# Sliding-window attention with a feed-forward block: batch 3's k moved from TensorE transposes to a transposing DMA

## The chip, the core and the metric

One core of a Trainium2 chip runs the whole kernel. Its engines each execute their own instructions in order: TensorE (PE in the profile; PEld is its weight load), VectorE (DVE), ScalarE (ACT), GpSimd (POOL) and SyncE (SP), which here only issues DMAs. The metric is the device time of one execution in microseconds (us); less is better. A measurement of this kernel can tell about 0.2% from no change.

## The reference

```python
# q, k, v: (8 batches, 8 heads, 576 tokens, 64)
scores = scale * np.matmul(q, k.transpose(0, 1, 3, 2))
mask = (rel >= 0) & (rel < 128)              # rel = query position - key position
scores = np.where(mask, scores - slopes * np.abs(rel), -1e9)
attn = softmax(scores); attn_out = np.matmul(attn, v)
x = attn_out.transpose(0, 2, 1, 3).reshape(4608, 512)
h = x @ w_in                                 # 512 -> 2048
g = h * np.clip(h + 3.0, 0.0, 6.0) / 6.0
return g @ w_out                             # 2048 -> 512
```

## The kernel before

**Units of work.** Attention is done for g = 0 to 31, a pair of heads each: g = 4 * batch + pair. The feed-forward block goes by tiles of 512 tokens (nt = 0 to 8): for each tile 16 "up" units (L532, four matmuls into hps, then ACT and DVE make gbuf) and 16 "down" units (L587, four matmuls into ops; every fourth ends a block of 128 rows, which DVE copies to osb and SyncE writes out, L597). Tile 3 covers tokens 1536 to 2047, that is the end of batch 2 and the most of batch 3. Four consecutive matmuls of an up unit read xT for head pairs 0, 1, 2, 3.

**Order.** The order on every engine is the order of the program, written by hand. `segment` runs iterations g = 8 to 32: scores(g) on TensorE, exp_diag and exp_off (ACT makes pd, po and p4buf, GpSimd masks them, L427, L436, L442), values(g - 1) (TensorE, then DVE divides into avs, L474), back(g - 1), stage_next(g), and between these `fill(n)`, which hands out n units of the feed-forward block. An up unit is only handed out once all pairs of its batches have been written to xT in the program's order.

**q and k.** Scores need q and k with the 64 channels of two heads on the partitions (qTb, kTb, two of each, by turns of the batch). There are two ways. By *doubles*: load_double (L105) brings runs of 9 tokens, GpSimd casts them (prepare_double, L246), TensorE transposes (double, L269, 5 and 4 transposes) and ACT or DVE copies the result (L271). By *token blocks and a transposing DMA*: load_block (L117) brings blocks of 128 tokens (five for a tensor, the last one half), GpSimd casts them into tbuf (cast_tokens, L213), and one transposing DMA, issued by SyncE (xbar, L218), writes qTb or kTb. Before the change batch 2 and batch 3's k go by doubles, batch 3's q and all of batches 4 to 7 by token blocks, with one tbuf for q and k.

**v and the values.** v is loaded by token blocks too and cast by GpSimd into vbuf (L206, L209). back(g) (L510) writes avs into xT by a transposing DMA on SyncE for g >= 8, other than g = 10 and 11, which go over TensorE and ACT (L517, L519).

**Queues.** All loads in the steady part, the transposing DMAs and the outputs leave through SyncE's one queue, in program order; a load whose room is not free, or a transposing DMA whose cast is not done, holds those behind it. Four ldbuf take turns: q3 is in ldbuf3, k3 in ldbuf1, v3 in ldbuf0. `LOADS` says in which iteration's stage_next a tensor is loaded ("q4" is batch 4's q).

Of the kernel before, what the change touches and what calls it, by code (L numbers as in the profile page):

```python
# [11 lines left out]
BF16 = mybir.dt.bfloat16  # L12
# [6 lines left out]
def kernel(  # L19
# [9 lines left out]
    nc = tc.nc  # L29
# [35 lines left out]
    held = ctx.enter_context(tc.tile_pool(name="held", bufs=1))  # L65
    prs = ctx.enter_context(tc.tile_pool(name="prs", bufs=2))
    ppool = ctx.enter_context(tc.tile_pool(name="ppool", bufs=2))
    small = ctx.enter_context(tc.tile_pool(name="small", bufs=2))
    rpool = ctx.enter_context(tc.tile_pool(name="rpool", bufs=2))
    opool = ctx.enter_context(tc.tile_pool(name="opool", bufs=4))  # L70
# [2 lines left out]
    ps_h = ctx.enter_context(tc.tile_pool(name="ps_h", bufs=2, space=bass.MemoryType.PSUM))  # L73
    ps_o = ctx.enter_context(tc.tile_pool(name="ps_o", bufs=1, space=bass.MemoryType.PSUM))

    tbuf = held.tile([128, NP, NQ, 128], BF16, name="tbuf")
    ldbuf = [held.tile([128, NQ * H * D], FP32, name=f"ldbuf{i}") for i in range(4)]
    gbuf = [held.tile([128, n_ms, NT], BF16, name=f"gbuf{i}") for i in range(2)]
    vbuf = [held.tile([128, NQ, H, W], BF16, name=f"vbuf{i}") for i in range(2)]
# [35 lines left out]
    def load_block(b, nm, j, eng):  # L115
        n = min(128, S - j * 128)
        eng.dma_start(out=tokens(b, nm)[:n, j, :, :],  # L117
                      in_=src_of[nm][b, :, ds(j * 128, n), :].rearrange("h p d -> p h d"))
# [32 lines left out]
    def memsets_later():  # L151
        for i in range(2):
            nc.gpsimd.memset(p4buf[i], 1.0)
        nc.gpsimd.memset(kTb[1][:, :, 4, LAST:128], 0.0)
        nc.gpsimd.memset(vbuf[1][:, :, :, D:W], 1.0)
        nc.gpsimd.memset(vbuf[1][64:128, 4, :, 0:D], 0.0)
        nc.gpsimd.memset(tbuf[64:128, :, 4, :], 0.0)

    def warm_up(n):
        w = ps_av.tile([128, 4, 128], FP32, tag="av", name="w")  # L160
# [41 lines left out]
    def cast_tokens(b, nm):  # L202
        s = ld[b, nm]
        if nm == "v":
            for lo in (0, 2):
                nc.gpsimd.tensor_copy(  # L206
                    out=vbuf[b % 2][:, lo:lo + 2, :, 0:D].rearrange("p j h d -> p (j h) d"),
                    in_=s[:, lo:lo + 2, :, :].rearrange("p j h d -> p (j h) d"))
            nc.gpsimd.tensor_copy(out=vbuf[b % 2][:LAST, 4, :, 0:D], in_=s[:LAST, 4, :, :])  # L209
            return  # L210
        for j in range(NQ):
            m = min(128, S - j * 128)
            nc.gpsimd.tensor_copy(out=tbuf[:m, :, j, :],  # L213
                                  in_=s[:m, j, :, :].rearrange("p (i e) d -> p i (e d)", e=2))

    def xbar(b, nm):
        dst = (qTb if nm == "q" else kTb)[b % 2]
        nc.sync.dma_start_transpose(out=dst.rearrange("p h j c -> p (h j) c"),  # L218
                                    in_=tbuf.rearrange("p h j c -> p (h j c)"))

    st = {}

# [243 lines left out]
    def values(g, qts):  # L466
        av = ps_av.tile([128, 3, 2, W], FP32, tag="av", name="av", padded_shape=[128, 3, 2, 85])
        nq = len(qts)
        av_matmuls(g, qts, lambda qt, e: av[:, qt - qts[0], e, :])
        if qts[0] == 0:  # L470
            st[g, "avs"] = small.tile([128, NQ, 2, D], BF16, tag="avs", name="avs")
        rc = small.tile([128, 3, 2, 1], FP32, tag="rc", name="rc")
        nc.vector.reciprocal(rc[:, 0:nq, :, :], av[:, 0:nq, :, D:W])
        nc.vector.tensor_tensor(  # L474
            out=st[g, "avs"][:, qts[0]:qts[0] + nq, :, :], in0=av[:, 0:nq, :, 0:D],
            in1=rc[:, 0:nq, :, :].to_broadcast([128, nq, 2, D]), op=ALU.mult)

    def attend(g):
        wide = score_banks()
        av = wide[:, :, 0:NQ * W].rearrange("p e (j c) -> p e j c", j=NQ)  # L480
        av_matmuls(g, range(NQ), lambda qt, e: av[:, e, qt, :])
        avs = st[g, "avs"] = small.tile([128, NQ, 2, D], BF16, tag="avs", name="avs")
        rc = small.tile([128, 2, NQ, 1], FP32, tag="rcw", name="rcw")
        nc.vector.reciprocal(rc, av[:, :, :, D:W])
        nc.vector.tensor_tensor(out=avs.rearrange("p j e d -> p e j d"), in0=av[:, :, :, 0:D],  # L485
                                in1=rc.to_broadcast([128, 2, NQ, D]), op=ALU.mult)

    def attend_split(g, tags):
        st[g, "avs"] = small.tile([128, NQ, 2, D], BF16, tag="avs", name="avs")
# [119 lines left out]
    def fill(n):  # L609
        for _ in range(n):  # L610
# [3 lines left out]
            if fn is moe_up and done[0] < NP * (min((nt * NT + NT - 1) // S, B - 1) + 1):  # L614
# [3 lines left out]

    V, P, A = nc.vector.tensor_copy, nc.gpsimd.tensor_copy, nc.scalar.copy

    LOADS = {9: "v3", 10: "q4", 12: "k4", 13: "v4", 14: "q5", 16: "k5", 17: "v5", 18: "q6",
             20: "k6", 21: "v6", 22: "q7", 24: "k7", 25: "v7"}

    VCAST = {15: 4, 19: 5, 23: 6, 27: 7}
# [1 line left out]
    def stage_next(g):  # L626
        b, hp = divmod(g, NP)
        nb = b + 1
        if g == 2 * NP:
            cast_tokens(2, "v")  # L630
        late = nb > 3 and hp == 1
        for n in LOADS.get(g, "").split():
            for j in range(3 if late else NQ):
                load_block(int(n[1]), n[0], j, nc.sync)
        if nb == 3 and hp < 2:
            prepare_double(3, hp, (P,), "k")
        if nb == 3 and hp == 1:
            cast_tokens(3, "q")
            xbar(3, "q")
        elif nb < B and nb > 3 and hp < 2:  # L640
            cast_tokens(nb, "qk"[hp])
            xbar(nb, "qk"[hp])
        for n in LOADS.get(g, "").split() if late else ():
            for j in range(3, NQ):
                load_block(int(n[1]), n[0], j, nc.sync)
        if VCAST.get(g):
            cast_tokens(VCAST[g], "v")

# [80 lines left out]
    def second_batch():  # L729
        scores_diag(NP + 0)  # L730
        exp_diag(NP + 0, 0)
        exp_diag(NP + 0, 1)
        up_begin(0, 2, n_ks, "av")
        scores_off(NP + 0)
        exp_off_full(NP + 0)
        wide_double(1, 1, "k", V)
        fill(2)
        scores_diag(NP + 1)
        exp_diag(NP + 1, 0)
        exp_diag(NP + 1, 1)  # L740
# [24 lines left out]
        load_w_out(2)  # L765
        load_w_out(3)
        prepare_double(2, 1, (P, P))
        nc.gpsimd.memset(ldbuf[2][:, 0:1], 0.0)
        load_tokens(2, "v")
        for dp in range(2):  # L770
            load_double(3, dp, "k", nc.sync)
        load_tokens(3, "q")
        up_begin(0, 13, n_ks)
        attend(NP + 1)
        back(NP, "o")
        attend(NP + 2)
# [17 lines left out]
    def segment(lo, hi, fills):  # L794
        for g in range(lo, hi + 1):
# [2 lines left out]
                done[0] = g - 1  # L798
            if lo < g < hi and g != 3 * NP + 1:
                scores(g)  # L800
            turn = {2 * NP: (2, 1, "k"), 2 * NP + 1: (2, 1, "q"),
                    2 * NP + 2: (3, 0, "k"), 2 * NP + 3: (3, 1, "k")}.get(g)
            if turn:
                double(*turn, 0, "av", A)
            fill(f[0])
            if turn:
                double(*turn, 1, *(("h", V) if turn[0] == 2 else ("av", A)))
            if g < hi:
                exp_diag(g, 0)
            fill(f[1])  # L810
# [76 lines left out]
```

## Time and profile before

| | |
|---|---|
| median of three runs | 319.51 us (319.5 to 320.04) |
| profiled execution | 319.64 us |
| its span in the profile | 317.9 us |
| TensorE busy | 307.0 us |
| SyncE transposing DMAs for q and k (L218) | 9, issue 3.7 to 4.8 us each |
| loads of 256 KB by token blocks | packets of 256 B |
| loads of 288 KB by doubles | packets of 2304 B |

All times below count from the start of the span; the execution's own time is 1.7 us longer. In a timeline, a row is: start, duration, engine, line and operation, what it writes and reads, how many were merged. The duration of a DMA row on SyncE is the time in which SyncE is occupied with issuing it, not the transfer; the trace also has a landing record for each DMA, the moment when its last part arrived. Iterations begin, by scores on TensorE, at 59.97 (g = 9), 67.98 (10), 75.90 (11), 84.11 (12), 88.03 (13), 96.04 (14), 103.21 (15), 111.24 (16) and 119.28 (17).

Landing records of the DMAs that the prediction speaks of (last part, us):

```
v2 blocks       58.02 58.97 60.05 61.23 62.06
k3, doubles     62.64 63.38 64.74 65.58
q3 blocks       66.79 68.05 70.39 71.93 72.79
v3 blocks       74.93 76.11 77.29 78.51 79.24
q3 transposed   82.77
back(9)         83.71
q4 blocks       85.72 86.82 88.02 89.42 89.76
k4 blocks       92.93 94.11 96.24 97.26 97.70
q4 transposed   99.98
k4 transposed   110.24
v4, last block  111.49
q5, last block  118.59
back(14)        120.47
back(15)        121.48
back(19)        153.26
```

### The profile page before, as it was taken

To read this page: it belongs to the slowest core of one execution; us is meant where nothing else is said; L and a number is where in the kernel's file an instruction comes from. 1 tells how busy PE (TensorE), PEld (TensorE's weight loads), DVE (VectorE), ACT (ScalarE), POOL (GpSimd) and SP (SyncE) were. 2 spreads that over 40 slices of the span, in tenths; PEclk is the share of its full clock that TensorE was granted. 3 is DMA by queue.
4 is the path that set the end of the run, shared out by engine and by line. 5 is a ranking of instruction groups with operands and counts; after the bars stand their busy time and mean duration, and the time that the engine had idled before them with its cause. 6 is when DMAs were issued, how large, how long until landed. Compare 5 with 4: busy or idle time off the path is not lost.

```text
span 317.9 us, 6980 instructions
## 1 busy us (share of the span) xinstructions
PE 307.0 (97%) x2671; PEld 163.4 (51%) x2710; DVE 176.1 (55%) x344; ACT 196.8 (62%) x338; POOL 138.9 (44%) x247
## 2 busy tenths in 40 slices
PE   8889999999999999999999999999999999999996
PEld 3565474455554445555676644454444444444443
DVE  6677676554456654566465546564656455455510
ACT  3869986877767666766667756675764244244401
POOL 7358192674594684548463854472231000000000
PEclk9999999999999999999999999999999999999999
DMA  7999999999999999999999999934112100000112
GB/s 271 264 373 215 255 236 200 236 235 198 216 265 180 222 215 212 213 196 253 186 178 219 190 206 198 228 95 57 49 29 75 66 34 33 35 33 33 66 57 77
DMA packets 131425, 52.43 MB, mean 165 GB/s; under 512 B 118976, under 2 KB 122816, under 8 KB 131392
## 3 DMA queue, kind: packets, MB, share of 16 engines
q1 hardware_dynamic: 125648, 46.15, 69.0%
q0 software_dynamic: 3696, 3.67, 7.1%
q10 hardware_dynamic: 2048, 2.16, 2.2%
q8 instruction: 21, 0.34, 0.5%
q14 instruction: 12, 0.10, 0.1%
HBM read 36.70 MB, written 9.44 MB: 145 GB/s over the span
## 4 chain that ended last, share of the span: by engine, by line
PE 90%; ACT 3%; DVE 3%; issue 2%; POOL 0%; DVEq 0%; POOLq 0%; ACTq 0%
PE hps L532 38%; PE ops L587 37%; PE score L399 3%; PE av L463 2%; PE av L455 2%; DVE avs L485 1%; PE ops L568 1%; PE w L163 1%; ACT w_out_sb L422 1%; PE score L346 1%; PE tp L269 1%; ACT r L556 1%; DVE gbuf L557 1%; PE score L301 1%; PE score L357 1%
## 5 line engine op out<-in xcount | busy, mean ns | idle before, releaser
L556 ACT ACTIVATE r<-hps,bias 128x512 f32<-128x512 f32 x144 | 98.9, 689 | 84.2 <-PE hps L532 83.9
L557 DVE SCALAR_TENSOR_TENSOR gbuf<-r,hps 128x512 bf16<-128x512 f32 x144 | 98.8, 688 | 91.6 <-ACT r L556 90.1
L532 PE MATMUL hps<-xT,w_in_sb 128*128 128x512 bf16 (+1 forms) x623 | 142.0, 358 | 1.7 <-ACT xT L519 0.3
L587 PE MATMUL ops<-w_out_sb,gbuf 128*128 128x512 bf16 x538 | 133.8, 379 | 2.3 <-issue 1.8
L532 PEld LDWEIGHTS <-w_in_sb 128*128 128x128 bf16 x640 | 59.2, 98 | 54.0 <-issue 1.5
L587 PEld LDWEIGHTS <-gbuf 128*128 128x128 bf16 x560 | 52.4, 98 | 57.5
L427 POOL TENSOR_SCALAR_AFFINE_SELECT pd<-pd 128x512 bf16<-128x512 bf16 x48 | 29.4, 631 | 35.2 <-ACT pd L425 35.2
L436 POOL TENSOR_SCALAR_AFFINE_SELECT po<-po 128x512 bf16<-128x512 bf16 x48 | 30.1, 633 | 30.8 <-ACT po L434 30.1
L596 DVE COPY osb<-ops 128x512 f32<-128x512 f32 x33 | 22.7, 688 | 23.8 <-PE ops L587 23.7
L425 ACT ACTIVATE pd<-score,bias_d 128x512 bf16<-128x512 f32 x48 | 31.1, 683 | 6.4 <-PE score L399 6.4
L434 ACT ACTIVATE po<-score,bias_o 128x512 bf16<-128x512 f32 x48 | 33.1, 690 | 0.0
L213 POOL CAST tbuf<-ldbuf 128x512 bf16<-128x512 f32 (+1 forms) x45 | 25.7, 611 | 15.7 <-issue 14.6
L474 DVE TENSOR_TENSOR avs<-av,rc 128x384 bf16<-128x384 f32 (+1 forms) x48 | 23.6, 491 | 1.6
L463 PEld LDWEIGHTS <-pd 128*128 128x128 bf16 x192 | 14.3, 97 | 8.2 <-issue 0.2
L455 PE MATMUL av<-vbuf,po 128*128 128x65 bf16 x192 | 18.0, 193 | 0.0
L206 POOL CAST vbuf<-ldbuf 128x1024 bf16<-128x1024 f32 x14 | 14.3, 1041 | 7.6 <-DMA ldbuf<-in_v_dram 7.6
L463 PE MATMUL av<-vbuf,pd 128*128 128x65 bf16 x192 | 17.3, 194 | 0.0
L455 PEld LDWEIGHTS <-po 128*128 128x128 bf16 x192 | 14.3, 98 | 3.0 <-DVE avs L474 0.5
L439 ACT ACTIVATE p4buf<-score,bias_d 128x64 bf16<-128x64 f32 x48 | 15.6, 324 | 0.0
L399 PEld LDWEIGHTS <-kTb 64*64 64x64 bf16 x480 | 9.4, 106 | 9.1 <-issue 8.5
L399 PE MATMUL score<-qTb,kTb 64*64 64x192 bf16 (+1 forms) x480 | 13.1, 234 | 0.0
L246 POOL CAST pr<-ldbuf 128x576 bf16<-128x576 f32 x18 | 11.5, 668 | 2.6 <-PE tp L238 1.3
(107 smaller groups left out, 201.7 us busy)
## 6 DMA issues: line engine op xcount, KB each, us to landing
out_dram<-osb SPq DMA_DIRECT2D x33, 256.0 KB, 3.5
ldbuf<-in_v_dram SPq DMA_DIRECT2D x31, 256.0 KB, 4.6
ldbuf<-in_q_dram SPq DMA_DIRECT2D x20, 256.0 KB, 5.0
ldbuf<-in_k_dram SPq DMA_DIRECT2D x16, 256.0 KB, 5.3
ldbuf<-in_q_dram SPq DMA_DIRECT2D x12, 288.0 KB, 6.6
ldbuf<-in_k_dram SPq DMA_DIRECT2D x12, 288.0 KB, 6.7
w_out_sb<-in_moe_w_out_dram POOLq DMA_DIRECT2D x4, 512.0 KB, 9.1
w_in_sb<-in_moe_w_in_dram POOLq DMA_DIRECT2D x3, 512.0 KB, 8.8
```

Source lines behind the costliest of these rows:

```text
L213: nc.gpsimd.tensor_copy(out=tbuf[:m, :, j, :], in_=s[:m, j, :, :].rearrange("p (i e) d -> p i (e d)", e=2))
L399: nc.tensor.matmul(wide[e][c, ds(at, n)], lhsT=kT[r, j, c], rhs=qT[r, ds(q0, n)], start=True, stop=True)
L425: nc.scalar.activation(out=pd[:, e, :, :], in_=block_scores(g, e, False), func=ACT.Exp, bias=bias_d[:, h:h + 1], scale=scale)
L427: nc.gpsimd.affine_select(out=pd[:, e, :, :], in_=pd[:, e, :, :], pattern=[[0, 4], [1, 128]], channel_multiplier=-1, base=0, compare_op=AL ...
L434: nc.scalar.activation(out=po[:, e, :, :], in_=sc, func=ACT.Exp, bias=bias_o[:, h:h + 1], scale=scale)
L436: nc.gpsimd.affine_select(out=po[:, e, :, :], in_=po[:, e, :, :], pattern=[[0, 4], [-1, 128]], channel_multiplier=1, base=-1, compare_op=A ...
L455: nc.tensor.matmul(out_av, lhsT=po[:, e, (qt if full(g) else qt - 1) % 4, :], rhs=vb[:, qt - 1, h, :], start=True, stop=False)
L463: nc.tensor.matmul(out_av, lhsT=d, rhs=vb[:, qt, h, :], start=(qt == 0), stop=True)
L532: nc.tensor.matmul(hps[:, lo:hi], lhsT=w_in_sb[:, ks, ts(ms, 128)], rhs=xT[:, ks, ds(src, hi - lo)], start=(ks == 0), stop=(ks == n_ks - 1))
L556: nc.scalar.activation(out=r6, in_=hps, func=ACT.Relu, bias=bias3[:, 0:1], scale=1.0 / 6.0)
L557: nc.vector.scalar_tensor_tensor(out=gts[nt][:, ms, :], in0=r6, scalar=1.0, in1=hps, op0=ALU.min, op1=ALU.mult)
L587: nc.tensor.matmul(ops[nt, sub], lhsT=gts[nt][:, ms, ts(sub, 128)], rhs=w_out_sb[:, ms, :], start=(ms == 0), stop=(ms == n_ms - 1))
```

## The change

Batch 3's k goes the way of the later batches: it is loaded by token blocks behind q3, cast in iteration 9 and transposed by a DMA; q3's cast and transposing DMA move from iteration 9 to iteration 8. The four transposing groups in iterations 10 and 11 are gone. q and k have a cast buffer each. avs, the normed values, come from a pool of three buffers instead of two. v3's loads move from iteration 9 to iteration 10, ahead of q4's, and k4's from iteration 12 to 11. In iteration 13 k4's transposing DMA now stands ahead of all of v4's loads (before: behind three of the five blocks); in iterations 17, 21 and 25 the order stays three blocks, transposing DMA, two blocks.

```diff
+    outs = ctx.enter_context(tc.tile_pool(name="outs", bufs=3))
...
-    tbuf = held.tile([128, NP, NQ, 128], BF16, name="tbuf")
+    tbuf = {nm: held.tile([128, NP, NQ, 128], BF16, name=f"tbuf{nm}") for nm in "qk"}
...
-        nc.gpsimd.memset(tbuf[64:128, :, 4, :], 0.0)
+        for nm in "qk":
+            nc.gpsimd.memset(tbuf[nm][64:128, :, 4, :], 0.0)
...
-            st[g, "avs"] = small.tile([128, NQ, 2, D], BF16, tag="avs", name="avs")
+            st[g, "avs"] = outs.tile([128, NQ, 2, D], BF16, tag="avs", name="avs")
...
-    LOADS = {9: "v3", 10: "q4", 12: "k4", 13: "v4", 14: "q5", 16: "k5", 17: "v5", 18: "q6",
+    AHEAD = {13: 0, 17: 3, 21: 3, 25: 3}
+
+    LOADS = {10: "v3 q4", 11: "k4", 13: "v4", 14: "q5", 16: "k5", 17: "v5", 18: "q6",
              20: "k6", 21: "v6", 22: "q7", 24: "k7", 25: "v7"}
...
-        late = nb > 3 and hp == 1
-        for n in LOADS.get(g, "").split():
-            for j in range(3 if late else NQ):
-                load_block(int(n[1]), n[0], j, nc.sync)
-        if nb == 3 and hp < 2:
-            prepare_double(3, hp, (P,), "k")
-        if nb == 3 and hp == 1:
-            cast_tokens(3, "q")
-            xbar(3, "q")
-        elif nb < B and nb > 3 and hp < 2:
+        loads = [(int(n[1]), n[0], j) for n in LOADS.get(g, "").split() for j in range(NQ)]
+        first = AHEAD.get(g, len(loads))
+        for load in loads[:first]:
+            load_block(*load, nc.sync)
+        if 3 <= nb < B and hp < 2:
             cast_tokens(nb, "qk"[hp])
             xbar(nb, "qk"[hp])
-        for n in LOADS.get(g, "").split() if late else ():
-            for j in range(3, NQ):
-                load_block(int(n[1]), n[0], j, nc.sync)
+        for load in loads[first:]:
+            load_block(*load, nc.sync)
...
-        for dp in range(2):
-            load_double(3, dp, "k", nc.sync)
         load_tokens(3, "q")
+        load_tokens(3, "k")
...
-            turn = {2 * NP: (2, 1, "k"), 2 * NP + 1: (2, 1, "q"),
-                    2 * NP + 2: (3, 0, "k"), 2 * NP + 3: (3, 1, "k")}.get(g)
+            turn = {2 * NP: (2, 1, "k"), 2 * NP + 1: (2, 1, "q")}.get(g)
...
-                double(*turn, 1, *(("h", V) if turn[0] == 2 else ("av", A)))
+                double(*turn, 1, "h", V)
```

More of the change, by code (lines that the diff above doesn't have):

```diff
@@ L212, in cast_tokens @@
             m = min(128, S - j * 128)
-            nc.gpsimd.tensor_copy(out=tbuf[:m, :, j, :],
+            nc.gpsimd.tensor_copy(out=tbuf[nm][:m, :, j, :],
                                   in_=s[:m, j, :, :].rearrange("p (i e) d -> p i (e d)", e=2))
@@ L218, in xbar @@
         nc.sync.dma_start_transpose(out=dst.rearrange("p h j c -> p (h j) c"),
-                                    in_=tbuf.rearrange("p h j c -> p (h j c)"))
+                                    in_=tbuf[nm].rearrange("p h j c -> p (h j c)"))
     st = {}
@@ L481, in attend @@
         av_matmuls(g, range(NQ), lambda qt, e: av[:, e, qt, :])
-        avs = st[g, "avs"] = small.tile([128, NQ, 2, D], BF16, tag="avs", name="avs")
+        avs = st[g, "avs"] = outs.tile([128, NQ, 2, D], BF16, tag="avs", name="avs")
         rc = small.tile([128, 2, NQ, 1], FP32, tag="rcw", name="rcw")
@@ L488, in attend_split @@
     def attend_split(g, tags):
-        st[g, "avs"] = small.tile([128, NQ, 2, D], BF16, tag="avs", name="avs")
+        st[g, "avs"] = outs.tile([128, NQ, 2, D], BF16, tag="avs", name="avs")
         for tag, qts in zip(tags, ((0, 1, 2), (3, 4))):
```

## The prediction

> **What bounds the kernel now.** I read the page first: busy shares, the slices and the chain that ended last.
>
> ```profile
> span 317.9 us, 6980 instructions
> PE 307.0 (97%) x2671; PEld 163.4 (51%) x2710; DVE 176.1 (55%) x344; ACT 196.8 (62%) x338; POOL 138.9 (44%) x247
> ...
> DMA  7999999999999999999999999934112100000112
> ...
> PE 90%; ACT 3%; DVE 3%; issue 2%; POOL 0%; DVEq 0%; POOLq 0%; ACTq 0%
> ```
>
> Two things are full at once: TensorE over the whole span, and the DMA engines in the first 65% of it (up to about 205 us). TensorE executes in order and is the chain; whatever it stops for is lost for good, and whatever it need not do is won. So I ask for each edit what TensorE sheds, and which of its waits comes to end last. Of the DMA side I read SyncE's own timeline, since nearly every DMA leaves through its one queue, in program order:
>
> ```profile
> 110.88 4.42 SPq L117 DMA_DIRECT2D ldbuf<-in_q_dram  x5
> 115.40 0.66 SPq L597 DMA_DIRECT2D out_dram<-osb  x1
> 116.16 1.26 SPq L510 DMA_TRANSPOSE xT<-avs  x1
> 117.51 0.53 SPq L597 DMA_DIRECT2D out_dram<-osb  x1
> 118.14 1.23 SPq L510 DMA_TRANSPOSE xT<-avs  x1
> 119.43 5.35 SPq L117 DMA_DIRECT2D ldbuf<-in_k_dram  x5
> ```
>
> Each starts where the one before ended. The first L510 here is back(14): its avs was complete at 109.2 (values(14) ends on TensorE at 108.7), and it left 7 us late, behind q5's loads. From 58.8 to 118 SyncE never stands free longer than 0.8 us. So this queue runs behind its program. The next view, TensorE's timeline, shows who would feel it:
>
> ```profile
> 119.28 0.55 PE L399 MATMUL score<-qTb,kTb 64*64 64x192 bf16 x20
> 119.99 1.67 PE L587 MATMUL ops<-w_out_sb,gbuf 128*128 128x512 bf16 x7 [0.16 <-issue]
> ...
> 121.80 1.89 PE L532 MATMUL hps<-xT,w_in_sb 128*128 128x512 bf16 x8
> ```
>
> Counting the units handed out by the fills, these eight are the first up-projections of token tile 3, the first to read batch 3's rows of xT. The fourth (ks = 3, at 121.80 + 3 x 0.216 = 122.45) reads what back(15) writes: the L510 at 118.14, which lands at 121.48 by its landing record (the last of its 16 completions). The slack is 0.9 us.
>
> **What TensorE sheds.** Batch 3's k goes no longer through PE: 2 x 9 transposes and four ACT copies in iterations 10 and 11.
>
> ```profile
> 67.98 0.55 PE L399 MATMUL score<-qTb,kTb 64*64 64x192 bf16 x20
> 68.46 0.45 PE L269 MATMUL tp<-ident,pr 128*128 128x128 bf16 x5
> 68.96 0.81 PE L587 MATMUL ops<-w_out_sb,gbuf 128*128 128x512 bf16 x3
> 69.75 0.38 PE L269 MATMUL tp<-ident,pr 128*128 128x128 bf16 x4
> 69.97 1.03 PE L532 MATMUL hps<-xT,w_in_sb 128*128 128x512 bf16 x4
> ```
>
> Nine transposes at about 0.056 us from start to start are 0.50 us. Beside them TensorE stands 0.14 us before the second group and 0.12 us before the values at 70.95, both on the av bank that ACT's copies (0.76 and 0.73 us, L271) are emptying. Together 0.76 us per iteration, 1.5 us for two, all on the path. Bounds: 1.0 (transposes alone) to 1.5. ACT's 2.97 us and GpSimd's four 576-wide casts (2.5 us) lie beside the path.
>
> **What goes into the queue.** k3 by token blocks: landings of v3's blocks (74.93, 76.11, 77.29, 78.51, 79.24) show about 1.2 us per 256 KB and 0.5 to 0.7 for the half one, so 5.3 us. The four loads they replace landed 3.5 us after v2's last (62.06 to 65.58). Net +1.8 us. One transposing DMA more: its issue holds SyncE 3.8 us (L218, 3.69 to 4.83); in a full stream it landed 2.2 us after its predecessor (q4's: 97.70, then 99.9). So +2.3 to +3.8. Added in all: 4.1 to 5.6 us of queue, between 58.8 and 91. v3's loads only change place, from ahead of q3's transposing DMA to behind back(9); the order k's transposing DMA before v's loads at iteration 13 moves back(15) not at all, as both stand before it. What can be won back before 118 are SyncE's own waits: 0.6 us (102.31 to 102.94, for k4's cast, which waited for the single tbuf) and 0.7 at 87.7 to 88.4; 0 to 1.3. **The lag at back(15) is 2.8 to 5.6 us; I take 4.4.** back(15) then lands at 125.9, and the fourth matmul of tile 3 starts at 125.9 + 0.1 for the semaphore = 126.0, against 122.45: **+3.5 us** (+1.9 to +4.7 by the ends; 0.65 more if the wait sits on the first of the four), whatever TensorE gained before.
>
> A walk through the queue gives the same. q3 lands from 62.06 on: 67.4 to 68.4; k3 72.8 to 74. A last block leaves SyncE some 3.7 us before it lands, so k3 is out at 69.1 to 70.3; q3's transposing DMA to 74, an output and back(8) to 76, k3's to 80, an output and back(9) to 82 (before: 82.05, as v3's loads stood there). Then v3 to 86.5, q4 to 91.3 where it ended at 86.5: 4.8 us late, and from there the same transfers as before.
>
> **Waits that appear earlier on.** They are not added: each only says when one matmul can start.
> - q3 is cast on GpSimd already in iteration 8, at 62.92, before its blocks land. Its last cast ends at 68 to 69; behind it stand iteration 9's four masks (0.59 us each): done at 70.4 to 71.3. values(9) is due at 70.95 - 0.76 = 70.2: +0.2 to +1.1 of stall.
> - scores(12), due at 82.6 to 83.5, needs k3's transposing DMA, issued to 80, landing 1.7 to 3 us later: 81.7 to 83. Just in time.
> - v3 lands at about 89.5 where q4 landed (89.76; v3 before: 79.24). Its cast stands on GpSimd ahead of iteration 12's masks: cast ends 90.7, the two po masks 91.9, and values(12) was at 91.08. So TensorE stands here at **+0.8 us** (+0.3 to +1.7) against before.
> - v4 lands 4.7 us later (116.2), its cast ends near 117, po(16)'s masks at 119.5, due at 121.5 or later: hidden. q5's cast ends at 123.6, values(17) is due at 129.5: hidden.
>
> The other edits: a cast buffer for each of q and k ends GpSimd's wait for the first transposing DMA (the 4 us before 100.09 and 130.50), where nothing waits for GpSimd: 0. One 0.52 us memset more at 6.4: its next cast (6.51 to 7.17) would end at 7.63, its transposes come at 7.90: 0, or 0.3 without that cover. Three avs buffers: before, back(14) lands at 120.47, and avs(16), in the same buffer, is written at 122.53; 4.4 us later that would stop DVE, with three it doesn't: 0 now. After iteration 17 TensorE is late by as much as the queue; the queue again finds 1 to 1.5 us of waits per batch (148.0 to 148.6, 133.0 to 133.4), so back(19) (landed 153.26, read from 153.95) should not stop TensorE again: 0, up to +1.
>
> **The Trainium skill** speaks to the price of the stall. Row: the granted clock shows 9 in all 40 slices, but in this kernel's first 7 us 512-wide matmuls come 0.43 us apart and later 0.216, so a start at half pace costs here what the clock row does not show. The Trainium skill, page "TensorE: Matmul & The Clock Gate", section "Part 1: The HAM clock gate", says that after an idle window of about 3.4 us the clock is halved until it has been busy as long. Were 3.5 us of the time after a stall spent at 0.43, 1.75 us more would go. My stalls are about 2.3 us by values(12) (the 1.5 shed and 0.8) and 2.7 at tile 3, near such a window but under it; so this is part of rival 3 and not in the sum.
>
> **Rivals.**
> 1. *Gain of 1.5 us: 318.0.* The queue's lag dies before it reaches TensorE. This needs back(15) to land by 120.9, earlier than now, that is the added work of 4 us to fall into gaps of the queue. For it: the landings have uneven stretches (q3's third block took 2.3 us instead of 1.2), and DMA's busy share includes waiting. Against it: back(14)'s 7 us of lateness. 0.16.
> 2. *Slower by 0.3 to 1.7: about 320.3.* The lag is mostly won back (under 1.8 us), and v3's lateness at values(12) decides alone. For it: GpSimd's cast order is certain. 0.14.
> 3. *More than the forecast, 325 to 328:* after a stall the first 3.5 us go at the start's pace of 0.43 us a matmul (+1.75), or GpSimd, waiting for later landings, stops TensorE again in batches 4 to 6. 0.12.
> 4. *The change does nothing to the end, 319.5:* shed and stall cancel. 0.03.
>
> **How the numbers follow.** The profiled execution took 319.64 us with a span of 317.9, the runs' median is 319.51; TensorE is the chain to the last instruction, so the shift at 122 us is the shift of the end: 319.5 + 3.5 = 323.0 (the forecast's own range, by the ends of the lag and 0.65 more, is 321.4 to 324.9; chance 0.55). The range must take in rival 2 below and part of rival 3 above: 319.8 to 325.8. A measurement of this kernel can tell about 0.2% (0.64 us). Faster by more: 0.16. Within: 0.03 and a fifth of rival 2, 0.06. Slower: 0.78.
>
> **What would show it.** Right: no L269 after 64 us; back(15) landing 3 us or more later; a TensorE gap of 1.5 to 4 us just before tile 3's first L532, put down to the xT DMA; a gap before values(12) put down to GpSimd's masks; SyncE without a pause to 125. Wrong: back(15) at 121.5 or before, or xT landing in time with TensorE gapless, total 318.

## The result and the profile after

The changed kernel takes 327.58 us in the median of four runs (327.0 to 328.91), the kernel before 319.77 beside it (319.5 to 320.15): a ratio of 1.0233, interval 1.0207 to 1.0259. The forecast was 323.0: the sign was right, the size was not. The profiled execution took 327.0 us with a span of 325.3, 7.4 more than before. In the changed kernel most lines are numbered two higher (block loads one): the up matmul is L534, the down L589, the values L457 and L465, scores L401, back L512, the transposing DMA for q and k L220, block loads L118, v's casts L208 and L211, GpSimd's po mask L438.

The page of the changed kernel, its head, slices of the DMA engines and chain:

```profile
span 325.3 us, 6959 instructions
PE 310.6 (95%) x2692; PEld 162.4 (50%) x2692; DVE 176.2 (54%) x344; ACT 194.7 (60%) x334; POOL 140.4 (43%) x249
...
DMA  7999999999999999998999999952131200000112
...
PE 80%; DMA 7%; SPq 4%; ACT 3%; DVE 2%; POOL 2%; issue 1%; POOLq 0%; DVEq 0%; ACTq 0%
```

TensorE is 97% of the old span and 95% of the new. The chain tells more: DMA and SyncE's queue, absent from it before, now hold 11%. TensorE's timeline shows where:

```profile
91.13 0.23 PE L465 MATMUL av<-vbuf,pd 128*128 128x65 bf16 x2
93.83 0.23 PE L457 MATMUL av<-vbuf,po 128*128 128x65 bf16 x1 [2.47 <-POOL po L438]
...
94.42 0.23 PE L457 MATMUL av<-vbuf,po 128*128 128x65 bf16 x1 [0.30 <-POOL po L438]
```

and 33 us later:

```profile
126.38 0.59 PE L534 MATMUL hps<-xT,w_in_sb 128*128 128x512 bf16 x2
128.82 0.38 PE L534 MATMUL hps<-xT,w_in_sb 128*128 128x512 bf16 x1 [1.85 <-DMA xT<-avs]
130.00 1.24 PE L534 MATMUL hps<-xT,w_in_sb 128*128 128x512 bf16 x5 [0.81 <-DMA xT<-avs]
```

The first stop is values(12), behind GpSimd's masks; the second is the start of tile 3: the third matmul waits for back(14) (landed 128.78), the fourth for back(15) (landed 129.96). The chain of waits, read just ahead of that matmul, says the same in order of time (start, duration, what):

```profile
125.46 4.50 DMA xT<-avs
129.96 0.04 issue
130.00 1.24 PE hps L534 x5
```

How late TensorE is against before, by the start of scores(g), from both traces:

```
g             8      11     12     14     17     18     31
after-before  +0.66  +0.81  +0.05  +4.57  +4.57  +7.55  +7.55
```

Iteration 11 shows the 0.76 shed by itself; iteration 10's was used up by the stand at values(9). After tile 3 the number doesn't move again: the end is late by what the fourth matmul of tile 3 is late, 130.00 - 122.45 = 7.55.

And SyncE's queue, in which back(15) is the last line shown:

```profile
64.96 6.60 SPq L118 DMA_DIRECT2D ldbuf<-in_k_dram  x5
71.73 3.59 SPq L220 DMA_TRANSPOSE qTb<-tbufq  x1
...
77.41 3.08 SPq L220 DMA_TRANSPOSE kTb<-tbufk  x1
...
82.88 5.04 SPq L118 DMA_DIRECT2D ldbuf<-in_v_dram  x5
87.97 5.94 SPq L118 DMA_DIRECT2D ldbuf<-in_q_dram  x5
...
125.46 1.23 SPq L512 DMA_TRANSPOSE xT<-avs  x1
```

k3's five loads and its transposing DMA are new; q4's loads leave at 87.97 instead of 82.11, and back(15) at 125.46 instead of 118.14. From 59.8 to there SyncE is never free for more than 0.5 us.

### The profile page after: what moved, and what is told of

It reads as the page before. It is cut to its first block, busy times and chain, and to the rows that moved or that the text cites. A ratio compares the mean times of both kernels' runs of the same rounds, so it can differ in the third digit from the quotient of the medians.

```text
span 325.3 us, 6959 instructions
## 1 busy us (share of the span) xinstructions
PE 310.6 (95%) x2692; PEld 162.4 (50%) x2692; DVE 176.2 (54%) x344; ACT 194.7 (60%) x334; POOL 140.4 (43%) x249
## 4 chain that ended last, share of the span: by engine, by line
PE 80%; DMA 7%; SPq 4%; ACT 3%; DVE 2%; POOL 2%; issue 1%; POOLq 0%; DVEq 0%; ACTq 0%
PE hps L534 35%; PE ops L589 34%; DMA ldbuf<-in_q_dram 4%; PE score L401 3%; SPq L118 2%; PE av L465 2%; DMA ldbuf<-in_v_dram 2%; PE av L457 2%; DMA xT<-avs 1%; PE ops L570 1%; PE score L465 1%; POOL po L438 1%; ACT r L558 1%; DVE gbuf L559 1%; ACT w_out_sb L424 1%
## 5 line engine op out<-in xcount | busy, mean ns | idle before, releaser
L534 PE MATMUL hps<-xT,w_in_sb 128*128 128x512 bf16 (+1 forms) x640 | 144.1, 359 | 3.2 <-DMA xT<-avs 2.7
L589 PE MATMUL ops<-w_out_sb,gbuf 128*128 128x512 bf16 x560 | 139.1, 381 | 0.0
L534 PEld LDWEIGHTS <-w_in_sb 128*128 128x128 bf16 x640 | 59.4, 98 | 58.1 <-issue 5.6
L589 PEld LDWEIGHTS <-gbuf 128*128 128x128 bf16 x560 | 52.4, 98 | 58.1 <-issue 0.5
L438 POOL TENSOR_SCALAR_AFFINE_SELECT po<-po 128x512 bf16<-128x512 bf16 x48 | 30.1, 633 | 34.2 <-ACT po L436 33.6
L457 PE MATMUL av<-vbuf,po 128*128 128x65 bf16 x192 | 18.5, 194 | 3.3 <-POOL po L438 3.3
L208 POOL CAST vbuf<-ldbuf 128x1024 bf16<-128x1024 f32 x14 | 14.4, 1041 | 14.1 <-DMA ldbuf<-in_v_dram 14.1
L465 PEld LDWEIGHTS <-pd 128*128 128x128 bf16 x192 | 14.6, 98 | 8.0
L465 PE MATMUL av<-vbuf,pd 128*128 128x65 bf16 x192 | 18.1, 195 | 0.0
L457 PEld LDWEIGHTS <-po 128*128 128x128 bf16 x192 | 14.5, 98 | 6.9 <-POOL po L438 3.8
L215 POOL CAST tbufq<-ldbuf 128x512 bf16<-128x512 f32 (+1 forms) x25 | 14.6, 610 | 4.2 <-DMA ldbuf<-in_q_dram 4.0
L215 POOL CAST tbufk<-ldbuf 128x512 bf16<-128x512 f32 (+1 forms) x25 | 14.4, 610 | 2.0 <-DMA ldbuf<-in_k_dram 1.9
L401 PEld LDWEIGHTS <-kTb 64*64 64x64 bf16 x480 | 9.4, 106 | 9.1 <-issue 8.5
L401 PE MATMUL score<-qTb,kTb 64*64 64x192 bf16 (+1 forms) x480 | 13.1, 234 | 0.0
```

Of the source, the lines that this page charges most:

```text
L215: nc.gpsimd.tensor_copy(out=tbuf[nm][:m, :, j, :], in_=s[:m, j, :, :].rearrange("p (i e) d -> p i (e d)", e=2))
L401: nc.tensor.matmul(wide[e][c, ds(at, n)], lhsT=kT[r, j, c], rhs=qT[r, ds(q0, n)], start=True, stop=True)
L438: nc.gpsimd.affine_select(out=po[:, e, :, :], in_=po[:, e, :, :], pattern=[[0, 4], [-1, 128]], channel_multiplier=1, base=-1, compare_op=A ...
L457: nc.tensor.matmul(out_av, lhsT=po[:, e, (qt if full(g) else qt - 1) % 4, :], rhs=vb[:, qt - 1, h, :], start=True, stop=False)
L465: nc.tensor.matmul(out_av, lhsT=d, rhs=vb[:, qt, h, :], start=(qt == 0), stop=True)
L534: nc.tensor.matmul(hps[:, lo:hi], lhsT=w_in_sb[:, ks, ts(ms, 128)], rhs=xT[:, ks, ds(src, hi - lo)], start=(ks == 0), stop=(ks == n_ks - 1))
```

## The experiments

Theory: the end is late because SyncE's queue is full, so that every transfer added delays back(15), which tile 3 reads. Rivals: values(12) with its stop and its slow clock sets the end; or masks behind later casts do; or the start-up does. Ratios are to the kernel before, run on the same chip.

```
                              median   ratio   interval          back(15): issued, landed
before               319.8 to 320.5                              118.14  121.48
after                         327.58   1.0233  1.0207 to 1.0259  125.46  129.96
e1_v3_early                   328.07   1.0241  1.0216 to 1.0266  123.25  128.62
e2_q_behind                   325.27   1.0154  1.0110 to 1.0199  121.21  123.58
e3_both                       324.09   1.0119  1.0075 to 1.0163  119.01  121.57
e4_no_k3_transpose            324.27   1.0105  1.0050 to 1.0159  120.73  125.94
e5_k3_loads_out               326.03   1.0173  1.0134 to 1.0212  121.39  126.53
e6_before_one_transpose_more  324.01   1.0102  1.0058 to 1.0146  121.42  124.75
e7_k3_by_doubles              321.61   1.0044  1.0024 to 1.0065  120.15  124.69
e8_spread                     340.68   1.0634  1.0572 to 1.0695
e9_before_one_memset_more     320.06   1.0002  0.9985 to 1.0020
e10_downs_first               325.28   1.0161  1.0135 to 1.0187  125.03  129.53
e11_memset_v3_downs           358.69   1.1203  1.1183 to 1.1222
e12_memset_later              327.21   1.0226  1.0180 to 1.0271  125.59  130.93
e13_buffers_and_order         320.47   1.0014  1.0004 to 1.0023  117.76  120.84
e14_before_no_k3              318.90   0.9961  0.9947 to 0.9974  117.42  120.53
e15_neither                   320.22   0.9993  0.9976 to 1.0010  118.95  123.52
```

**Is it values(12) or back(15)?** v3's loads go right behind k3's transposing DMA, ahead of back(8) and back(9):

```diff
-    AHEAD = {13: 0, 17: 3, 21: 3, 25: 3}
+    AHEAD = {9: 0, 13: 0, 17: 3, 21: 3, 25: 3}
-    LOADS = {10: "v3 q4", 11: "k4",
+    LOADS = {9: "v3", 10: "q4", 11: "k4",
...
-            if g > lo and by_xbar(g - 1):
+            if g > lo and by_xbar(g - 1) and g != 9:
                 back(g - 1)
             fill(f[5])
             if g < hi:
                 stage_next(g)
+            if g == 9:
+                back(g - 1)
```

> The changed kernel with v3's loads right behind k3's transposing DMA and ahead of back(8) and back(9), so that they leave SyncE some 3 us earlier; what stands ahead of back(15) in the queue stays the same in sum. Queue theory (the sum of what SyncE's queue must move ahead of back(15) sets the end): the stall at values(12) and the 2.5 us at half clock behind it go, back(15) still lands at about 130, tile 3 waits for all of it: 327.0 us (326.3 to 328). Rival (v3's lateness with the half clock behind it has a price of its own, 4.5 us, that adds to the rest): 323.1 us.

The stop at values(12) is gone, TensorE is only 1.0 to 1.2 late from g = 14 to 17 instead of 4.6, and the end is as late as in the changed kernel. Everything came out again at tile 3:

```profile
126.43 0.38 PE L534 MATMUL hps<-xT,w_in_sb 128*128 128x512 bf16 x1 [2.88 <-DMA xT<-avs]
128.66 1.87 PE L534 MATMUL hps<-xT,w_in_sb 128*128 128x512 bf16 x4 [1.86 <-DMA xT<-avs]
```

The four matmuls behind the stop take 1.87 us, about 0.45 each: here the clock was halved. So removing the stop at values(12), large as it looks, wins nothing at the end. That the two ends agree so closely is partly luck: back(15) landed 1.34 earlier than in the changed kernel, so that tile 3's fourth matmul was 6.2 late, and the slow clock behind this longer stop added the rest of the 8.8 by which the profiled execution ends late. The edit also has a price of its own: back(8), now behind v3, lands at 88.14, and avs(11) reuses its buffer. DVE shows it, a third avs buffer notwithstanding:

```profile
88.23 0.56 DVE L476 TENSOR_TENSOR avs<-av,rc 128x384 bf16<-128x384 f32 x1 [1.56 <-DMA xT<-avs]
```

**Is it the queue ahead of back(15)?** q5's, q6's and q7's loads go behind it; then both edits together.

```diff
-    LOADS = {10: "v3 q4", 11: "k4", 13: "v4", 14: "q5", 16: "k5", 17: "v5", 18: "q6",
-             20: "k6", 21: "v6", 22: "q7", 24: "k7", 25: "v7"}
+    LOADS = {10: "v3 q4", 11: "k4", 13: "v4", 16: "q5 k5", 17: "v5",
+             20: "q6 k6", 21: "v6", 24: "q7 k7", 25: "v7"}
```

> The changed kernel with the q loads of batches 5, 6 and 7 moved from two iterations ahead of back(15), back(19), back(23) to just behind them; v3 is left late. Queue theory: back(14) and back(15) leave 5 us earlier, land by 125, tile 3 does not wait; the stall at values(12) and its half clock stay: 324.6 us (324 to 325.3). Rival (the loads taken from ahead of back(15) are only put off and stop TensorE later, at q5's cast or at back(19)): 326 us or more.

> Both edits together: v3 early and the q loads behind back(15), back(19), back(23). Queue theory: neither wait is left, the 1.5 us that TensorE sheds comes through, less some 0.9 at values(9): 320 us (319.0 to 321). Rival (the DMA engines are simply full, and the lateness comes out at some other reader): 322 us or more.

back(15) lands at 123.58 and 121.57, and the wait at tile 3 is gone in both. e2 gains 2.3 us by it. e3 has neither stop and still takes 324.1, so its expectation of 320 fell: the lateness comes out at the next place. TensorE's timeline of e3 in iteration 18:

```profile
130.68 0.20 PE L465 MATMUL av<-vbuf,pd 128*128 128x65 bf16 x1 [0.42 <-POOL pd L429]
131.26 0.20 PE L465 MATMUL av<-vbuf,pd 128*128 128x65 bf16 x1 [0.38 <-POOL pd L429]
131.85 0.20 PE L457 MATMUL av<-vbuf,po 128*128 128x65 bf16 x1 [0.38 <-POOL po L438]
```

These are values(17), matmul by matmul behind masks that stand on GpSimd behind q5's late casts. In e3 the reader of the loads that were put off waits instead; that no other order would do better is not shown.

**What is each added transfer worth?** The changed kernel without k3's transposing DMA (batch 3's scores then read batch 1's k); without four of k3's five block loads (its cast reads what lay in the buffer); and without both.

```diff
-            xbar(nb, "qk"[hp])
+            if (nb, hp) != (3, 1):
+                xbar(nb, "qk"[hp])
```

```diff
-        load_tokens(3, "k")
+        load_block(3, "k", 4, nc.sync)
```

> The changed kernel without k3's transposing DMA (left out of the work: batch 3's scores then read batch 1's k). k3 is still loaded and cast. Queue theory: all behind it leaves 3 to 3.8 us earlier; v3 lands by 88.5, values(12) waits under 1 us, back(15) lands at 126 to 127: 323.9 us (323 to 325). Rival (such a transfer costs the stream only the 2.2 us between landings): back(15) at 127.8, 325.4 us.

> The changed kernel with four of k3's five token-block loads left out of the work (batch 3's k is then made of what the buffer held). Four transfers of 1.2 us less in the queue. Queue theory: v3 lands by 87.5, values(12) hardly waits, back(15) lands at about 125.2 instead of 129.96, tile 3 waits for it: 322.6 us, or up to 324.9 if the clock halves after that wait as it did without k3's transposing DMA. Rival (the price of k3's way is the transposing DMA and its cast alone, the loads fall into gaps): 327 us.

> The changed kernel without the transposing DMA of batch 3's k and without four of the five loads of its blocks (its cast reads what lay in the buffer, batch 3's scores read batch 1's k): all that the change adds to the queue but one half block is out. The two left out alone brought back(15) 4.0 and 3.4 us earlier. Theory: the two add up, back(15) lands at 122.6 (122 to 123.2), TensorE, which is 0.8 ahead, waits about 1 us at tile 3 and keeps a clock of 1.00, and the end is at 319.8 to 320.8. Rival: they share one lateness (a queue that runs late by what GpSimd's casts allow): back(15) lands at 124.5 or later, the end is at 322 or more.

Without both, the change is even with before (0.9993, 0.9976 to 1.0010), although back(15) landed at 123.52, 0.3 outside what was expected. e5 missed its expectation: back(15) landed 1.3 later than forecast, and 326.0 is above the 324.9 that was allowed for a slow clock. In e15 the rest of TensorE's wait at tile 3 is 1.1 us:

```profile
123.57 1.24 PE L534 MATMUL hps<-xT,w_in_sb 128*128 128x512 bf16 x5 [1.11 <-DMA xT<-avs]
```

So about 7.4 us (327.58 - 320.22) hang on these two. For the size of each I take the queue's length, from the first load behind v2's to the issue of back(15), which leaves the start-up out:

```
before                   118.14 - 58.86 = 59.28
e15, neither             118.95 - 59.87 = 59.08
e4, the loads alone      120.73 - 59.12 = 61.61   +2.53
e5, transposing alone    121.39 - 59.43 = 61.96   +2.88
after, both              125.46 - 59.82 = 65.64   +6.56
```

Alone they cost 2.5 and 2.9, together 6.6: 1.15 more than the sum. Each length is from one execution, and equal queues differ by almost as much: 66.62 in e10 and 67.38 in e12 against the 65.64, and 60.88 in e9 against the 59.28. So a single price is good to some 1.7 us, and that the two cost more together than apart is likely, but not shown by these lengths alone. Four block loads occupy SyncE for some 7 us (36.5 for all loads of this stretch in e4, 29.2 in e15) and cost only 2.5, because in e15 SyncE stands free from 65.59 to 69.28, ahead of q3's transposing DMA. Of the 1.15, 1.0 arises ahead of v3's loads (from the same start to their issue: 17.22 in e15, 19.64 in e4, 19.63 in e5, 23.06 with both; 23.23, 23.61 and 23.88 in e10, e2 and e12, which have both too). There e15 has 0.78 free at 75.06, ahead of back(9). The loads alone leave nothing of it, the transposing DMA alone 0.23, ahead of itself; both together can use it once, and the changed kernel stands 0.50 again at that place (81.12). This fits the excess, and no run tests it.

**The same price in the kernel before.** One transposing DMA more, from tbuf into a spare tile, behind q3's:

```diff
             xbar(3, "q")
+            nc.sync.dma_start_transpose(out=spare.rearrange("p h j c -> p (h j) c"),
+                                        in_=tbuf.rearrange("p h j c -> p (h j c)"))
```

> The kernel before with one transposing DMA more, behind q3's in iteration 9, from q's cast buffer into a spare tile that nobody reads. Nothing else changes, nothing is shed. Queue theory: all behind it is 3 to 4 us late, back(15) lands at 124.5 to 125.5, tile 3 waits 2 to 3 us: 322.3 us (321.5 to 323), up to 2.3 more if the clock halves. Rival (the queue before the change has room for it): 319.8 us, no change.

back(15) is issued 3.3 later and lands 3.3 later: a price of that size holds in the other kernel. The place did not: the end was set 16 us earlier, at values(14), because with one tbuf GpSimd stands still until q4's transposing DMA lands, and k4's five casts then stand ahead of the masks. Its GpSimd timeline:

```profile
103.47 2.84 POOL L214 CAST tbuf<-ldbuf 128x512 bf16<-128x512 f32 x5 [7.46 <-DMA qTb<-tbuf]
106.26 1.22 POOL L428 TENSOR_SCALAR_AFFINE_SELECT pd<-pd 128x512 bf16<-128x512 bf16 x2
```

**The other parts, and what TensorE sheds.** First the change with k3 left on doubles, its casts, transposes and copies with it, and q3 cast in iteration 9; then the kernel before with the change's buffers and iteration 13's order alone; then the kernel before with batch 3's k left out altogether, loads, casts, transposes and copies (its scores read batch 1's k), the shed without its price.

```diff
-        load_tokens(3, "k")
+        for dp in range(2):
+            load_double(3, dp, "k", nc.sync)
```

```diff
-            for j in range(3 if late else NQ):
+            for j in range(0 if g == 13 else 3 if late else NQ):
```

```diff
-        for dp in range(2):
-            load_double(3, dp, "k", nc.sync)
...
-            turn = {2 * NP: (2, 1, "k"), 2 * NP + 1: (2, 1, "q"),
-                    2 * NP + 2: (3, 0, "k"), 2 * NP + 3: (3, 1, "k")}.get(g)
+            turn = {2 * NP: (2, 1, "k"), 2 * NP + 1: (2, 1, "q")}.get(g)
```

> The changed kernel with batch 3's k by doubles and q3's cast and transposing DMA in iteration 9 as before, all other parts of the change kept: two cast buffers, three avs buffers, v3's loads in iteration 10, k4's in 11, k4's transposing DMA ahead of all of v4's loads. Queue theory: the queue's sum ahead of back(15) is that of before, v3 lands at 86 to 87: 320.1 us (319.6 to 320.8). Rival (the new order of loads, with v3 late, costs by itself): 322 us or more.

> The kernel before with only the other edits: a cast buffer each for q and k, three avs buffers, and in iteration 13 k's transposing DMA ahead of all of v's loads. k3 stays with doubles, q3 and v3 stay where they were. Theory (the prediction's, which priced these edits at nothing): within 0.3 us of the kernel before; SyncE's and GpSimd's waits for the single buffer go, but nobody on the path waited for them. Rival: the edits move the queue: k4's cast no longer waits for q4's transposing DMA, back(15) lands up to 1.3 earlier or v4's loads shift something later; the time changes by 0.6 us or more in either direction.

> The kernel before with batch 3's k left out altogether: no loads by doubles, no casts, none of the 18 transposes and four copies of iterations 10 and 11; batch 3's scores read batch 1's k. This is the change with its added side free of charge. Theory (the prediction's shed): TensorE is 1.5 us ahead from iteration 12 on, nothing else waits, the time is 318.0 to 318.4. Rival: the shed 1.5 us is taken back by a wait that lay beside TensorE until now (values(12), or the fourth up matmul of tile 3, which had 0.9 of slack): 319 or more.

e14: TensorE goes from 0.52 late at g = 10 to 1.00 early at g = 12, a shed of 1.52; the end gains 1.2 us (0.8 to 1.7), less than the 1.5 expected, as 0.36 went again in iteration 15. So moving k3 off TensorE can win some 1.2 to 1.5 us here. e13: the edits that I priced at nothing cost 0.45 us (0.1 to 0.7), in the profiled execution all of it in the start-up: +0.46 at g = 8 and +0.47 at g = 31. e7, above the 320.8 expected: putting v3's loads behind back(9) leaves SyncE without work from 70.45 to 73.39, where it waits for q3's cast; back(15) comes 3.2 late, TensorE waits 1.09 at tile 3, and the time is up by 0.4% though nothing was added to the queue.

**Does tile 3 wait for the read of xT?** The queue untouched, tile 3 alone begins with eight down units instead of four:

```diff
-             ("DDDD",) * 4]
+             ("DDDD",) * 4,
+             ("DDDDDDDD", "UUD" * 8)]
...
-        for c in "".join(ORDER[0 if nt == 1 else 2 if nt == n_nt else 1]):
+        for c in "".join(ORDER[{1: 0, 3: 3, n_nt: 2}.get(nt, 1)]):
```

> The changed kernel, in which token tile 3 alone hands out eight down units of tile 2 ahead of its first up unit, instead of four. SyncE's queue is as in the changed kernel, so back(15) lands at about 130 again; TensorE has four down units (4 x 0.86 = 3.4 us) to do where it stood for 2.7 us before the up units. Queue theory: the gaps of 1.85 and 0.81 are gone, and the end comes 2.1 to 2.7 us earlier: 324.9 to 325.5 (a stand for a bank of ops between two tiles may take some 0.3 of it). Rival: the lateness does not come from the read of xT but from something that comes later on anyway (masks behind the later casts), as in the run with v3's loads early and q5 to q7 behind: 327.0 or more.

back(15) lands at 129.53, as late as before, and no up matmul waits: TensorE does down units in that time, after a stand of 0.48 at the bank of ops. From g = 17 to 18 it loses 0.64 instead of 2.98. The median is 2.3 us lower, within what the theory gave. The profiled execution, the slowest of the four, ends only 0.6 earlier than the changed kernel's: the new order of units costs it 1.85 again from g = 20 to 21, most of it where TensorE waits for a bank of ops:

```profile
126.75 2.75 PE L589 MATMUL ops<-w_out_sb,gbuf 128*128 128x512 bf16 x12 [0.48 <-DVE osb L598]
...
156.59 1.67 PE L589 MATMUL ops<-w_out_sb,gbuf 128*128 128x512 bf16 x7 [1.44 <-DVE osb L598]
```

**The start-up.** One memset more in the kernel before, and the changed kernel with the second memset moved to the opening of batch 2:

```diff
         nc.gpsimd.memset(tbuf[64:128, :, 4, :], 0.0)
+        nc.gpsimd.memset(spare[64:128, :, 4, :], 0.0)
```

> The kernel before with one 64x512 memset more on GpSimd at the start, beside tbuf's, into a tile that nothing reads; all else as before, the output too. In the changed kernel TensorE's iteration 8 began 0.66 us late, and in the other kernels with two memsets 0.49 to 1.03 late, while the kernel before with one transposing DMA more and one memset began it 0.08 early. Theory: the second memset (0.52 us) pushes GpSimd's first cast and with it TensorE: iteration 8 begins 0.4 to 0.7 late, and the time is 319.9 to 320.4 where the kernel before takes 319.7. Rival (the prediction's): it lies beside other work, iteration 8 begins within 0.2 of before, and the time is that of before.

> The changed kernel with only the second memset moved, from the start-up to the opening of batch 2. Theory: iteration 8 begins 0.5 to 0.7 earlier, SyncE's queue (whose pace follows the casts at the start) stays earlier by as much down to back(15), and the end is 0.5 to 0.7 earlier: 326.9 to 327.1. Rival: the queue is set by the transfers, not by the start, back(15) lands at 130.0 as before, and the end is that of the changed kernel, 327.6.

Both say that the memset is not it: with it the kernel before is 0.23 late at g = 8 and its time the same; without it the changed kernel is 0.92 late at g = 8. The start moved between -0.08 and +1.03 from one profiled execution to the next (+0.66, +0.60 and +0.89 in the changed kernel, e10 and e2, which do the same work up to there); what moves it was not settled. The median of e12 lies between its two expectations and can't tell them apart. e12 is also the run with the longest stop: it lost 2.3 at values(12) instead of 4.5, came to tile 3 at 124.5, and met back(14) at 129.74 and back(15) at 130.93.

```profile
129.78 0.59 PE L533 MATMUL hps<-xT,w_in_sb 128*128 128x512 bf16 x1 [5.25 <-DMA xT<-avs]
130.97 2.29 PE L533 MATMUL hps<-xT,w_in_sb 128*128 128x512 bf16 x5 [0.61 <-DMA xT<-avs]
```

Five matmuls in 2.29 us: a slow clock on top. Its runs lie between 325.8 and 330.5.

**Two attempts at a better version** failed, both on what an order of units asks of the other engines. e8 is e3 with the casts of batches 5 to 7 one iteration later and tile 2 beginning with six downs; e11 is e1 with the second memset moved and every tile from 3 on beginning with twelve.

```diff
-        if 3 <= nb < B and hp < 2:
-            cast_tokens(nb, "qk"[hp])
-            xbar(nb, "qk"[hp])
+        at = hp - (nb > 4)
+        if 3 <= nb < B and at in (0, 1):
+            cast_tokens(nb, "qk"[at])
+            xbar(nb, "qk"[at])
```

```diff
+             ("D" * 12, "UUUUD" * 4)]
...
-        for c in "".join(ORDER[0 if nt == 1 else 2 if nt == n_nt else 1]):
+        for c in "".join(ORDER[{1: 0, 2: 1, n_nt: 2}.get(nt, 3)]):
```

> The changed kernel with v3 early, the q loads behind back(15), back(19), back(23), the q and k casts and transposing DMAs of batches 5 to 7 one iteration later (so that GpSimd's masks no longer stand behind a cast that waits for its load), and two more down units of tile 1 ahead of values(12). Queue theory: no wait at tile 3, under 0.5 us at values(12), none at values(17): 319.6 us (318.8 to 320.6). Rival (the lateness comes out elsewhere again): 322 us or more.

> The changed kernel with three edits: v3's loads right behind k's transposing DMA of iteration 9 (ahead of back(8) and back(9)), the second memset moved out of the start-up into the opening of batch 2, and in tiles 3 to 8 twelve down units ahead of the first up unit. Queue theory: the stand at values(12) falls from 2.8 to some 1.5, with no half clock there (-1.4); iteration 8 begins 0.6 earlier; tile 3's wait for back(15) of 2.7 is gone, as twelve down units more than cover it; in all about 320.5 to 322. Rival: up units bunched behind the downs wait for ACT and for the banks of hps and ops in each of the six tiles, and give it back: 323 to 327.

In e8 the transposing DMA for k now leaves too late for scores(20), 24 and 28. In e11 there is no wait for xT, but up units four in a row outrun ACT and DVE, and downs twelve in a row the banks of ops: TensorE's idle time by line is 15.7 us at the ups and 18.2 at the downs, from then on in every tile.

```profile
149.20 0.59 PE L401 MATMUL score<-qTb,kTb 64*64 64x192 bf16 x20 [3.55 <-DMA kTb<-tbufk]
```

```profile
L533 PE MATMUL hps<-xT,w_in_sb 128*128 128x512 bf16 (+1 forms) x623 | 141.0, 357 | 15.7 <-DVE gbuf L558 13.0 <-ACT xT L520 0.3
L588 PE MATMUL ops<-w_out_sb,gbuf 128*128 128x512 bf16 x538 | 130.1, 379 | 18.2 <-DVE osb L597 15.6 <-issue 2.2
```

No kernel here that computes the whole reference beats the one before.

## Why the prediction was right in its place and wrong in its size

- **Right:** the sign; TensorE's shed (1.5 forecast, 1.52 in e14); that the end is set where tile 3's fourth matmul reads what back(15) wrote (e1 and e10 from two sides); that SyncE has no pause; the stands at values(9) and values(12) behind GpSimd's masks.
- **The step that failed:** "The lag at back(15) is 2.8 to 5.6 us; I take 4.4." It was 129.96 - 121.48 = 8.48. By the queue's lengths above: 0.96 for the start of the stretch (59.82 against 58.86; e10 and e12 started it at 58.41 and 58.21, so no run shows it as a price of the change), -0.20 for all other edits (e15), 2.53 for the loads (1.8 forecast), 2.88 for the transposing DMA (2.3 to 3.8 forecast), 1.15 beyond the sum of the two, and 1.16 because back(15) took 4.50 from issue to landing instead of 3.34. Each is from one profiled execution. The single prices were near; what was put at nothing is what the additions do to the transfers behind them. The prediction's walk through the queue shows the place: it had SyncE through with q4's loads at 91.3, 4.8 late, and SyncE was through at 93.91, 7.4 late. Of these 2.6, 0.9 had come up ahead of v3's loads (82.88 for 82); the rest is that the loads of v3 and q4 held SyncE 5.04 and 5.94 instead of 4.5 and 4.8. From there to back(15) it took as long as before (31.55 and 31.63), as the walk had it, and SyncE's own waits were won back as forecast (those over 0.2 us: 1.97 before, 0.50 after). Why v3's and q4's loads held SyncE longer, and why back(15) was longer under way, was not tried.
- **From lag to end** the working held: 8.48 less the slack of 0.9 is 7.55, and 319.77 + 7.55 = 327.3, against 327.58.
- **values(12):** 2.8 us of stop instead of 0.8. v3 landed at 92.26, not 89.5: 1.4 of it because its last load left SyncE later than in the walk, and 1.0 because of one part in sixteen (the other fifteen of its last block had landed by 91.22). GpSimd's timeline shows its cast and the masks behind it:

```profile
91.60 1.04 POOL L208 CAST vbuf<-ldbuf 128x1024 bf16<-128x1024 f32 x1 [2.13 <-DMA ldbuf<-in_v_dram]
92.58 0.61 POOL L211 CAST vbuf<-ldbuf 64x512 bf16<-64x512 f32 x1
93.15 1.22 POOL L438 TENSOR_SCALAR_AFFINE_SELECT po<-po 128x512 bf16<-128x512 bf16 x2
```

- **Rival 3** named the right figure by the wrong way. A slow clock did come, in the stretches after values(12) (start and end, length, busy time by engine, granted clock, DMA share, GB/s):

```profile
91.00:94.70 3.70, 0.93 (x12) 0.53 (x11) 1.38 (x2) 2.67 (x6) 3.10 (x6) 0.88 1.15 208
94.70:96.00 1.30, 1.30 (x8) 0.48 (x6) 0.75 (x2) 0.00 (x0) 1.24 (x3) 0.50 1.02 234
96.00:97.00 1.00, 1.00 (x4) 0.45 (x3) 0.00 (x0) 0.00 (x0) 0.39 (x1) 0.50 1.06 334
...
126.90:130.00 3.10, 0.45 (x2) 0.10 (x1) 0.73 (x3) 0.00 (x0) 1.16 (x2) 1.00 1.20 172
130.00:131.50 1.50, 1.50 (x7) 0.68 (x7) 0.36 (x1) 1.08 (x2) 0.00 (x0) 1.00 1.33 219
```

It cost TensorE some 1.4 us there, and the end nothing, since tile 3 waited anyway; behind tile 3's stop the clock stayed at 1.00. That holds for the profiled execution: its mean clock is 0.995, as in one other, and 0.990 in the remaining two, about twice as much time at the slow clock. In e1, e4, e5 and e12, where the stop at tile 3 was longer, it came there and reached the end: e1's row 130.00:131.00 and e4's 126.00:127.00 show 0.50, and e1's end lies 1.2 beyond the changed kernel's (a span of 326.5 against 325.3) though its back(15) landed 1.34 earlier. The Trainium skill, page "TensorE: Matmul & The Clock Gate", section "Part 1: The HAM clock gate", gives an idle window of about 3.4 us for this, which runs freely. The traces fit a window of that length that runs freely, and not one that has to be empty. The clock was low for 3.41 us at a time, or twice that. Laid end to end from a fall, stretches of 3.41 us tell the falls from the rest: in the eleven falls within the spans of these runs TensorE stood 2.05 (e6) to 3.41 us of the stretch that ended with the fall, and in the same runs, past their first 12 us, at most 1.71 of any other. In the changed kernel the clock fell at 93.81, after 2.46 us of stand, and the stop of 0.30 came later; at tile 3 TensorE stood 2.66 in all (1.85 and 0.81), but these fall into two stretches, 0.97 in one and 1.68 in the other, and the clock stayed. So the prediction's "near such a window but under it" was no reason to leave a slow clock out of the sum: where the stretches lie decides too, and the mean clocks of 0.995 and 0.990 show that it differs between executions of one kernel.

- **Hidden edits:** "0" for the buffers and the memset: 0.45 us (e13), in the profiled execution at the start, and not by the memset (e9).

## What to carry to other kernels

In a queue that never rests, price an added transfer by everything behind it up to the first reader on the critical path, and count each free moment of the queue once: two additions that each fit into the same gap can cost more together than apart. Let the transfers behind an addition become slower too, and compare several executions before reading a price of 1 us off one trace. A stop early on the critical path can cost nothing when a later one is set by the queue, so trace the end back from the last wait that is never caught up, not from the largest. Before moving work off a full engine, find the most that it can win (here 1.2 to 1.5 us, by leaving it out) and hold it against what the other full resource has to pay.

## What the runs showed of the hardware

- A transposing DMA for one tensor holds SyncE 3.0 to 5.4 us over all these runs, and lengthened the queue by 2.9 us where the queue had free time, and by 4.0 (65.64 - 61.61) where it had none; each of these two lengths is from a pair of single executions.
- The parts of one transposing DMA of xT mostly land within 0.2 us, but at times 1.7 apart: back(14) of the changed kernel 127.10 to 128.78, back(15) of e15 121.77 to 123.52. What holds the last part was not tried.
- The granted clock fell to 0.50 at the end of stretches of 3.41 us in which TensorE stood 2.05 us or more, and not where it stood 1.71 or less, the stretches laid end to end. It stayed low for one such stretch where TensorE stood at most 0.52 us of it, and for two where it stood 1.34 or more (e1, e4, e12 and once in e8).
- TensorE's start of iteration 8, some 50 us in, varies by up to 1.0 us between profiled executions with the same start-up work (-0.08 to +0.92 with one early memset, +0.23 to +1.03 with two).
